# Attention and mixture of depths on one core: group 0's 1/rms by a ScalarE square root and a Newton step instead of GpSimd's power

## The chip, the core and the metric

The kernel runs on 1 core of one Trainium2 chip, in float32. The metric is the device time of one execution in microseconds (us), as the median of several runs. A core has five engines with queues of their own, each worked off in order: PE (TensorE, matrix products, with weight loads listed as PEld), DVE (VectorE), ACT (ScalarE), POOL (GpSimd) and SP (SyncE, which issues most DMAs). They wait for each other through semaphores only.

## What is computed

Normalized attention over 8 batches and 12 heads of 448 tokens with 64 dimensions, then a mixture-of-depths layer on the 768 joined columns. Cut to what matters here:

```python
def rmsnorm(x, g):
    rms = np.sqrt(np.mean(x * x, axis=-1, keepdims=True) + 1e-06)
    return x / rms * g
q_n, k_n = (rmsnorm(q, g_q), rmsnorm(k, g_k))
scale = 1.0 / np.sqrt(q.shape[-1])
scores = scale * np.matmul(q_n, k_n.transpose(0, 1, 3, 2))
scores = scores - np.max(scores, axis=-1, keepdims=True)
attn = np.exp(scores)
attn = attn / (np.sum(attn, axis=-1, keepdims=True) + 1e-09)
return np.matmul(attn, v).astype(np.float32)
...
for b in range(B):                       # x: attention output as (8, 448, 768)
    top_idx = np.argpartition(-scores[b], capacity)[:capacity]   # scores = x @ w_gate
    xe = x[b, top_idx]
    ye = np.maximum(xe @ w1, 0.0) @ w2
    out[b, top_idx] = x[b, top_idx] + g[:, None] * ye            # g = sigmoid(scores)
```

Each query and key row needs 1/sqrt(mean of squares + 1e-6). This is the quantity that the change computes in another way, for the first group only.

## The kernel before

The 96 heads are worked off in 24 groups of four (three groups to a batch). A group's 448 keys are cut into 7 blocks of 64, and one block of one group is a unit, numbered u = 7 n + i. For a unit, `scores` (L320) multiplies 64 keys with all queries of the four heads on PE into two PSUM tiles (`sc`, four buffers, hence two units at a time), and ScalarE takes the exponential of each out of PSUM (L337), with the keys' 1/rms as its per-row scale; no maximum is taken off. `values` (L345) multiplies the result with v and adds up over the 7 units. `add_probs` (L368) adds the exponentials on VectorE for the denominators.

The order of all work is written out by hand. The main loop at the end of `fast` issues, for each round q of four units, the scores of two units, the values of earlier units, then tasks and slots: `at(slot, fn)` puts a piece of work into the slot of a unit, `task(when, fn)` puts it at an opening. Each engine's queue holds its part in that order.

1/rms is made for each group from token-major copies of queries (i = 0) and keys (i = 1), the `tok` tiles of 448 KB. `squares` (L242) squares 128x896 elements on ScalarE into one of two buffers `sq`, whose 65th column holds 1e-6; `sum_squares` (L250) adds each row's 65 elements on VectorE (L255) and raises the sums to -0.5 on GpSimd (L256). For group 0's queries both work in two halves. The keys' result goes to the exponential as it is. The queries' result must lie along the free dimension: for groups 0 and 1, `scale_q_early` (L291) spreads it with 28 small products against an identity on PE (L298) into two `sc` tiles, and VectorE multiplies the transposed queries `qT` with it and with `gg`, the product of the two gains and the scale (L307). Later groups go through DRAM (`rows_out`, `rows_in`, L287).

The start, in program order: `Loads.__init__` (L29) sends the gain columns on ScalarE's queue and the first tokens and queries on SP's, and runs one small Exp (L40). `_build` (L1411) compares the gains with a bound on VectorE and all engines branch on the outcome (L1434 to L1436). `fast` then fills the `sq` columns, builds the identity on GpSimd, issues nine more loads on SP, builds `pick_pair` (a selection matrix for the denominators' products at L396) and `gg` on VectorE, and runs 13 transposes of the identity on PE (L169), whose result nobody reads. Then come group 0's squares and powers, group 1's squares, `scale_q_early(0)`, group 1's sums and powers, and the main loop, whose first opening holds `scale_q_early(1)`, after the scores of units 0 to 3 and the values of units 0 and 1. `prepare(n, slot)` places the squares and sums of groups 2 and up; those of group 2 lie in slots 0 to 3.

SP's queue works in order too: a load into a `tok` buffer waits until the squares of the tile that held it are done, and everything behind it on SP waits with it.

Of the kernel before, what the change touches and what calls it, by code (L numbers as in the profile page):

```python
# [10 lines left out]
F32 = mybir.dt.float32  # L11
I32 = mybir.dt.int32
AF = mybir.ActivationFunctionType
OP = mybir.AluOpType
AX = mybir.AxisListType
# [10 lines left out]
class Loads:  # L26


    def __init__(self, nc, pool, qT, kT, vp, tok, g2):  # L29
        self.nc, self.pool = nc, pool  # L30
        self.src = {"tok": tok, "qT": qT, "kT": kT, "v": vp}
        self.tiles = {}
        self.groups = tok.shape[1]
        self.gcol = pool.tile([128, 2], F32, name="gcol", bufs=1)
        nc.scalar.dma_start(out=self.gcol, in_=g2)
        neg_half = pool.tile([128, 1], F32, name="neg_half", bufs=1)
        nc.vector.memset(neg_half, -0.5)

        warm = pool.tile([128, 1], F32, name="warm", bufs=1)
        nc.scalar.activation(out=warm, in_=neg_half, func=AF.Exp)  # L40
        self.neg_half = neg_half
        self.load("tok", 0, 0)
        self.load("tok", 0, 1)
        self.load("qT", 0)

    def load(self, name, n, i=None):
        b, g = divmod(n, self.groups)
        src = self.src[name]
        if i is not None:
            src = src[b, g, :, i]  # L50
        elif name == "v":
            src = src[b, g]
        else:
            src = src[b, 2 * g : 2 * g + 2].rearrange("c p s -> p c s")
        pool = self.v_pool if name == "v" else self.pool
        bufs = {"tok": 6, "qT": 4, "kT": 3, "v": 3}[name]
        held = [key for key in self.tiles if key[0] == name]
        if len(held) == bufs:
            del self.tiles[held[0]]
        t = pool.tile(list(src.shape), F32, name=name, bufs=bufs)  # L60
        self.nc.sync.dma_start(out=t, in_=src)
        self.tiles[name, n, i] = t

    def get(self, name, n, i=None):
# [4 lines left out]
def fast(  # L69
# [21 lines left out]
    nc = tc.nc  # L91

    B, NP, _, S = loads.src["qT"].shape
    CP = 112
    NJ = S // CP
    D = 64
    NI = S // D
# [11 lines left out]
    scale = 1.0 / math.sqrt(D)  # L109
# [25 lines left out]
    sss, rinvs, bcs = {}, {}, {}  # L135
# [17 lines left out]
    load("v", 1)  # L153

    gg = const.tile([128, 1], F32, name="gg")

    pick_pair = const.tile([128, NJ // 2, 32], F32, name="pick_pair")
    nc.vector.memset(pick_pair, 0.0)
    for jj in range(NJ // 2):
        for c in range(2):  # L160
            r = 2 * jj + c
            nc.vector.memset(pick_pair[D * c : D * (c + 1), jj, r : r + 1], 1.0)
    nc.vector.scalar_tensor_tensor(
        out=gg, in0=loads.gcol[:, 0:1], scalar=scale, in1=loads.gcol[:, 1:2], op0=OP.mult, op1=OP.mult
    )

    ps = ps_moe.tile([128, 512], F32, tag="moe", name="warm_ps")
    for _ in range(13):
        nc.tensor.transpose(out=ps[:, 0:128], in_=ident, identity=ident)  # L169

    wg = const.tile([CP, DM], F32, name="wg")
# [70 lines left out]
    def squares(n, i):  # L242
# [4 lines left out]
        sss[n, i] = norm_pool.tile([128, 2, NI], F32, name="ss", bufs=4)  # L247
        return sq

    def sum_squares(n, i, sq):  # L250
        ss = sss.pop((n, i))
        rinv = norm_pool.tile([128, 2, NI], F32, name="rinv", bufs=8)
        flat = "p h i -> p (h i)"
        for h in [slice(0, 1), slice(1, 2)] if (n, i) == (0, 0) else [slice(0, 2)]:
            nc.vector.tensor_reduce(out=ss[:, h], in_=sq[:, h], axis=AX.X, op=OP.add)  # L255
            nc.gpsimd.tensor_tensor(  # L256
                out=rinv[:, h].rearrange(flat),
                in0=ss[:, h].rearrange(flat),
                in1=neg_half.to_broadcast([128, (h.stop - h.start) * NI]),
                op=OP.pow,  # L260
            )
        rinvs[n, i] = rinv

    def rows_out(n):
# [616 lines left out]
        while late:  # L881
            add_probs(late.pop(0))

    for i in range(2):
        sum_squares(0, i, squares(0, i))
    later = [squares(1, i) for i in range(2)]
    scale_q_early(0)
    for i in range(2):
        sum_squares(1, i, later[i])
    task((0, 0), scale_q_early, 1)  # L890

    def run(slots):
# [35 lines left out]
    while done < len(groups) or tasks:  # L928
        now[:] = q, 0
        k = PER * q  # L930
        for half in range(HALVES):
            for u in (k + 2 * half, k + 2 * half + 1):
                if u < units:
                    scores(u)
            run_values(k + 2 * half - 1, q)
        opening(q, 0)
        for half in range(HALVES):
            slots = (k + 2 * half, k + 2 * half + 1)
            early = bool(late)
            if early:  # L940
                spare[0] = True
                opening(q, 1)
                spare[0] = False
                add_late()
            if not short(q):
                run(slots)
            some = piece(q)
            spare[0] = not some and half == 0
            if not early and (some or half == 0 or len(tasks) > 2):
                opening(q, half + 1)  # L950
            spare[0] = False
            run(slots)
        q += 1
# [535 lines left out]
```

## Time and profile before

| What | us |
|---|---|
| Median of 3 runs | 518.45 (517.85 to 519.04) |
| The profiled execution | 513.42 |
| Its span, first to last instruction | 511.7 |
| PE busy | 491.6 (96%) |
| DVE busy | 354.0 (69%) |
| ACT busy | 274.8 (54%) |
| POOL busy | 187.0 (37%) |
| POOL powers L256, 49 of them | 135.7, of 128x14 2.83 each |
| ACT exponentials L337, 336 of them | 186.0, 0.641 each |
| ACT squares L246, 49 of them | 45.9, 0.949 each |
| DVE sums L255, 49 of them | 52.1, 1.074 each |
| HBM | 84.37 MB read, 28.50 MB written |

Busy times are sums over the whole span. PE's are modelled at their ends, so a PE that is busy throughout need not be at its peak. Every time in a timeline is counted from the first instruction of the span; a line there gives the start, the duration, the engine, the line of the code, the operation, output and input by name, the number of instructions merged into it, and in brackets how long the engine had been idle and what ended that.

### The profile page before, as it was taken

The page shows a single profiled execution, that of the slowest core. Times are in us where ns is not written, and L with a number is a line of the kernel's source. Part 1 is how long each engine was busy: PE and PEld are TensorE (multiplying, and loading weights), DVE is VectorE, ACT ScalarE, POOL GpSimd, SP SyncE. Part 2 cuts the span into 40 slices and gives each one's busy share as a digit, 9 for nine tenths or more (in the row PEclk, how much of TensorE's full clock was granted, in tenths as well). Part 3 has the DMA queues.
Part 4 walks back from the last instruction along what each step waited for, and adds up shares of the span by engine and source line. Part 5 has one row for each costly group of instructions (what it writes and reads, how often), then busy time and mean ns, then how long its engine had stood idle before and what let it go on. Part 6 is the DMA issues. An engine that isn't in the chain of part 4 may idle for free. (4 is left out here: it accounts for less than half of the span.)

```text
span 511.7 us, 11121 instructions
## 1 busy us (share of the span) xinstructions
PE 491.6 (96%) x4429; PEld 279.4 (55%) x4429; DVE 354.0 (69%) x670; ACT 274.8 (54%) x507; POOL 187.0 (37%) x104
## 2 busy tenths in 40 slices
PE   5999999988999999999999999999999899999994
PEld 4544445435555444666654454665554454786683
DVE  4566898699866898996687886777567686623201
ACT  4787886866757466665454737654634536310000
POOL 4694548444524174427123085036220022020102
PEclk9999999999999999999999999999999999999998
DMA  8977889999964673899461989567423318232601
GB/s 294 387 247 257 271 272 365 326 296 319 283 204 129 214 248 121 283 323 331 134 201 26 350 280 302 190 191 207 136 72 88 110 38 260 89 109 58 221 3 36
DMA packets 49295, 105.82 MB, mean 207 GB/s; under 512 B 11571, under 2 KB 26420, under 8 KB 49234
## 3 DMA queue, kind: packets, MB, share of 16 engines
q1 hardware_dynamic: 45826, 98.70, 59.9%
q0 software_dynamic: 3264, 6.31, 3.7%
q8 instruction: 37, 0.61, 0.5%
q14 instruction: 24, 0.20, 0.1%
q10 hardware_dynamic: 144, 0.00, 0.0%
HBM read 84.37 MB, written 28.50 MB: 221 GB/s over the span
## 5 line engine op out<-in xcount | busy, mean ns | idle before, releaser
L337 ACT ACTIVATE p<-sc,rinv 128x448 f32<-128x448 f32 x336 | 186.0, 641 | 88.3 <-PE sc L328 74.3
L256 POOL TENSOR_TENSOR rinv<-ss,neg_half 128x14 f32<-128x14 f32 (+1 forms) x49 | 135.7, 2775 | 184.4 <-DVE ss L255 164.9
L328 PE MATMUL sc<-qT,kT 64*64 64x448 f32 x1344 | 152.7, 545 | 1.0 <-DVE qT L307 0.8
L352 PE MATMUL av<-p,v 64*64 64x448 f32 x1344 | 147.0, 537 | 0.0
L368 DVE TENSOR_TENSOR sum<-sum,p 128x896 f32<-128x896 f32 x107 | 116.5, 1089 | 8.1 <-ACT p L337 1.9
L352 PEld LDWEIGHTS av<-p,v 64*64 64x64 f32 x1344 | 57.6, 133 | 69.6 <-issue 62.3
L328 PEld LDWEIGHTS sc<-qT,kT 64*64 64x64 f32 x1344 | 52.5, 132 | 69.3 <-issue 43.8
L255 DVE TENSOR_REDUCE ss<-sq 128x14 f32<-128x910 f32 (+1 forms) x49 | 52.1, 1074 | 11.9 <-ACT sq L246 11.6
L639 PE MATMUL moe_ps<-xeT,w 128*128 128x256 f32 (+1 forms) x288 | 56.1, 347 | 0.0
L539 POOL DMA_INDIRECT selected<-x,rank x32 | 35.8, 1118 | 47.7 <-DVE x L531 39.7
L639 PEld LDWEIGHTS moe_ps<-xeT,w 128*128 128x128 f32 x288 | 46.2, 191 | 6.8 <-issue 2.6
L246 ACT ACTIVATE sq<-tok 128x896 f32<-128x896 f32 (+1 forms) x49 | 45.9, 949 | 5.9 <-DMA tok<-in_tok_dram 5.6
L443 DVE TENSOR_TENSOR x<-x_ps,rden 112x512 f32<-112x512 f32 x48 | 32.5, 687 | 20.8 <-PE x_ps L441 18.3
L467 DVE SCALAR_TENSOR_TENSOR prod<-x,wg 112x256 f32<-112x256 f32 x96 | 40.6, 423 | 2.9
L587 POOL DMA_INDIRECT out_dram<-xe,row x10 | 10.5, 1052 | 85.7 <-DVE xe L596 67.9
L639 PE MATMUL sc<-xeT,w 128*128 128x256 f32 (+1 forms) x192 | 32.2, 328 | 0.3 <-ACT xeT L615 0.3
L441 PE MATMUL x_ps<-ident,xT 128*112 128x128 f32 x192 | 28.8, 276 | 2.0 <-DVE x L443 2.0
L639 PEld LDWEIGHTS sc<-xeT,w 128*128 128x128 f32 x192 | 28.8, 191 | 2.8 <-ACT xeT L615 0.5
L287 DVE SCALAR_TENSOR_TENSOR qT<-qT,gg,bc 128x896 f32<-128x896 f32 x22 | 25.3, 1149 | 4.4 <-DMA bc<-rows 4.4
L512 DVE SCALAR_TENSOR_TENSOR cmp<-score_rows,gate,earlier 112x448 f32<-112x448 f32 x32 | 21.9, 684 | 9.1 <-ACT score_rows L502 8.1
L441 PEld LDWEIGHTS x_ps<-ident,xT 128*112 128x112 f32 x192 | 21.8, 134 | 10.3 <-issue 4.5
L368 DVE TENSOR_TENSOR sum<-p 128x896 f32<-128x896 f32 x24 | 25.9, 1078 | 1.8 <-ACT p L337 1.8
(87 smaller groups left out, 331.9 us busy)
## 6 DMA issues: line engine op xcount, KB each, us to landing
tok<-in_tok_dram SPq DMA_DIRECT2D x48, 448.0 KB, 6.6
qT<-in_qT_dram SPq DMA_DIRECT2D x24, 448.0 KB, 6.6
kT<-in_kT_dram SPq DMA_DIRECT2D x24, 448.0 KB, 7.1
v<-in_vp_dram SPq DMA_DIRECT2D x24, 448.0 KB, 7.6
out_dram<-x SPq DMA_DIRECT2D x8, 1344.0 KB, 9.0
bc<-rows SPq DMA_DIRECT2D x44, 224.0 KB, 6.4
ring<-mixed SPq DMA_DIRECT2D x22, 384.0 KB, 5.3
xe<-selected SPq DMA_DIRECT2D x8, 385.0 KB, 3.7
```

The source lines that it names most:

```text
L246: nc.scalar.activation(out=sq[:, h, :, 0:D], in_=t[:, h], func=AF.Square, scale=scale)
L255: nc.vector.tensor_reduce(out=ss[:, h], in_=sq[:, h], axis=AX.X, op=OP.add)
L256: nc.gpsimd.tensor_tensor(out=rinv[:, h].rearrange(flat), in0=ss[:, h].rearrange(flat), in1=neg_half.to_broadcast([128, (h.stop - h.start) ...
L328: nc.tensor.matmul(out=scs[hh][D * c : D * (c + 1), 0:S], lhsT=get("kT", n)[r, c, D * i : D * (i + 1)], rhs=get("qT", n)[r, c, :], start=True,
L337: nc.scalar.activation(out=p[:, hh], in_=scs[hh][:, 0:S], func=AF.Exp, scale=rinvs[n, 1][:, hh, i : i + 1],)
L352: nc.tensor.matmul(out=avs[n][c][D * hh : D * (hh + 1), 0:S], lhsT=get("v", n)[r, hh, i, :], rhs=probs[u][r, hh], start=(i == 0), stop=(i ...
L368: nc.vector.tensor_tensor(out=sums[n], in0=probs.pop(u - 1) if begins else sums[n], in1=probs.pop(u), op=OP.add)
L441: nc.tensor.transpose(out=ps[:CP, j, :], in_=t[:, j, :], identity=ident)
L443: nc.vector.tensor_tensor(out=xs[b][:, :, col : col + 128].rearrange("p j (h d) -> p j h d", d=D), in0=ps[:CP].rearrange("p j (h d) -> p j ...
L467: nc.vector.scalar_tensor_tensor(out=prod[:, 0 : GH * D], in0=xs[b][:, j, cols], scalar=1.0, in1=wg[:, cols], op0=OP.mult, op1=OP.mult, ac ...
L539: w = nc.gpsimd.indirect_dma_start(out=t[:, :], out_offset=bass.IndirectOffsetOnAxis(ap=rank[:, j : j + 1], axis=0), in_=x[:, j, :], in_of ...
L639: nc.tensor.matmul(out=ps[:, i, :, :n], lhsT=w1[:, dc, 128 * (f0 + i) : 128 * (f0 + i + 1)], rhs=xeT[:, dc, 0:G, :n], start=(dc == 0), sto ...
```

## The change

For group 0 alone, the two powers on GpSimd (three instructions) are replaced. `sum_first` adds the squares as before; `root_first` takes the square root of the sums on ScalarE; `invert_first` takes its reciprocal on VectorE, y, and does one Newton step, y (1.5 - 0.5 s y y), in three more VectorE instructions. The small activation at the start is a Sqrt instead of an Exp. The first `tok` tile is loaded in two halves, the first on ScalarE's queue as its first instruction, the second on SP's. `pick_pair` and `gg` are built later, and there are 9 transposes at the start instead of 13. Group 1's squares, sums and powers no longer stand before the main loop but in it: queries behind the scores of unit 0, keys behind those of unit 2.

```diff
--- before.py
+++ after.py
@@ -32,14 +32,15 @@
         self.tiles = {}
         self.groups = tok.shape[1]
         self.gcol = pool.tile([128, 2], F32, name="gcol", bufs=1)
+        self.load("tok", 0, 0)
         nc.scalar.dma_start(out=self.gcol, in_=g2)
         neg_half = pool.tile([128, 1], F32, name="neg_half", bufs=1)
         nc.vector.memset(neg_half, -0.5)
 
-        warm = pool.tile([128, 1], F32, name="warm", bufs=1)
-        nc.scalar.activation(out=warm, in_=neg_half, func=AF.Exp)
+        warm = pool.tile([128, 2], F32, name="warm", bufs=1)
+        nc.vector.memset(warm, 1.0)
+        nc.scalar.activation(out=warm[:, 0:1], in_=warm[:, 1:2], func=AF.Sqrt)
         self.neg_half = neg_half
-        self.load("tok", 0, 0)
         self.load("tok", 0, 1)
         self.load("qT", 0)
 
@@ -58,7 +59,11 @@
         if len(held) == bufs:
             del self.tiles[held[0]]
         t = pool.tile(list(src.shape), F32, name=name, bufs=bufs)
-        self.nc.sync.dma_start(out=t, in_=src)
+        if (name, n, i) == ("tok", 0, 0):
+            for h, queue in enumerate((self.nc.scalar, self.nc.sync)):
+                queue.dma_start(out=t[:, h], in_=src[:, h])
+        else:
+            self.nc.sync.dma_start(out=t, in_=src)
         self.tiles[name, n, i] = t
 
     def get(self, name, n, i=None):
@@ -153,19 +158,9 @@
     load("v", 1)
 
     gg = const.tile([128, 1], F32, name="gg")
-
     pick_pair = const.tile([128, NJ // 2, 32], F32, name="pick_pair")
-    nc.vector.memset(pick_pair, 0.0)
-    for jj in range(NJ // 2):
-        for c in range(2):
-            r = 2 * jj + c
-            nc.vector.memset(pick_pair[D * c : D * (c + 1), jj, r : r + 1], 1.0)
-    nc.vector.scalar_tensor_tensor(
-        out=gg, in0=loads.gcol[:, 0:1], scalar=scale, in1=loads.gcol[:, 1:2], op0=OP.mult, op1=OP.mult
-    )
-
     ps = ps_moe.tile([128, 512], F32, tag="moe", name="warm_ps")
-    for _ in range(13):
+    for _ in range(9):
         nc.tensor.transpose(out=ps[:, 0:128], in_=ident, identity=ident)
 
     wg = const.tile([CP, DM], F32, name="wg")
@@ -247,18 +242,41 @@
         sss[n, i] = norm_pool.tile([128, 2, NI], F32, name="ss", bufs=4)
         return sq
 
+    def sum_first(i, sq):
+        ss = sss[0, i]
+        for h in [slice(0, 1), slice(1, 2)] if i == 0 else [slice(0, 2)]:
+            nc.vector.tensor_reduce(out=ss[:, h], in_=sq[:, h], axis=AX.X, op=OP.add)
+
+    def root_first(i):
+        root = norm_pool.tile([128, 2, NI], F32, name="ss", bufs=4)
+        nc.scalar.activation(out=root, in_=sss[0, i], func=AF.Sqrt)
+        return root
+
+    def invert_first(i, root):
+
+        ss = sss.pop((0, i))
+        rinv = norm_pool.tile([128, 2, NI], F32, name="rinv", bufs=8)
+        nc.vector.reciprocal(out=root, in_=root)
+        nc.vector.scalar_tensor_tensor(
+            out=rinv, in0=root, scalar=-0.5, in1=ss, op0=OP.mult, op1=OP.mult
+        )
+        nc.vector.tensor_tensor(out=rinv, in0=rinv, in1=root, op=OP.mult)
+        nc.vector.scalar_tensor_tensor(
+            out=rinv, in0=rinv, scalar=1.5, in1=root, op0=OP.add, op1=OP.mult
+        )
+        rinvs[0, i] = rinv
+
     def sum_squares(n, i, sq):
         ss = sss.pop((n, i))
         rinv = norm_pool.tile([128, 2, NI], F32, name="rinv", bufs=8)
         flat = "p h i -> p (h i)"
-        for h in [slice(0, 1), slice(1, 2)] if (n, i) == (0, 0) else [slice(0, 2)]:
-            nc.vector.tensor_reduce(out=ss[:, h], in_=sq[:, h], axis=AX.X, op=OP.add)
-            nc.gpsimd.tensor_tensor(
-                out=rinv[:, h].rearrange(flat),
-                in0=ss[:, h].rearrange(flat),
-                in1=neg_half.to_broadcast([128, (h.stop - h.start) * NI]),
-                op=OP.pow,
-            )
+        nc.vector.tensor_reduce(out=ss, in_=sq, axis=AX.X, op=OP.add)
+        nc.gpsimd.tensor_tensor(
+            out=rinv.rearrange(flat),
+            in0=ss.rearrange(flat),
+            in1=neg_half.to_broadcast([128, 2 * NI]),
+            op=OP.pow,
+        )
         rinvs[n, i] = rinv
 
     def rows_out(n):
@@ -881,12 +899,23 @@
         while late:
             add_probs(late.pop(0))
 
-    for i in range(2):
-        sum_squares(0, i, squares(0, i))
-    later = [squares(1, i) for i in range(2)]
+    sum_first(0, squares(0, 0))
+    root = root_first(0)
+    keys = squares(0, 1)
+    nc.vector.scalar_tensor_tensor(
+        out=gg, in0=loads.gcol[:, 0:1], scalar=scale, in1=loads.gcol[:, 1:2], op0=OP.mult, op1=OP.mult
+    )
+    invert_first(0, root)
+    sum_first(1, keys)
+    root = root_first(1)
     scale_q_early(0)
-    for i in range(2):
-        sum_squares(1, i, later[i])
+    invert_first(1, root)
+    nc.vector.memset(pick_pair, 0.0)
+    for jj in range(NJ // 2):
+        for c in range(2):
+            r = 2 * jj + c
+            nc.vector.memset(pick_pair[D * c : D * (c + 1), jj, r : r + 1], 1.0)
+    following = {0: (1, 0), 2: (1, 1)}
     task((0, 0), scale_q_early, 1)
 
     def run(slots):
@@ -932,6 +961,8 @@
             for u in (k + 2 * half, k + 2 * half + 1):
                 if u < units:
                     scores(u)
+                if u in following:
+                    sum_squares(*following[u], squares(*following[u]))
             run_values(k + 2 * half - 1, q)
         opening(q, 0)
         for half in range(HALVES):
```

## What I predict

> **What bounds the kernel now.** I read the windows by stage first, then the start in order of time, then the waits. The chain that ended last covers only the closing 8 us and says nothing about the start.
>
> ```profile
> core 0: us, PE busy (x) PEld busy (x) DVE busy (x) ACT busy (x) POOL busy (x), PEclk, DMA share, GB/s
> 0.00:13.00 13.00, 7.36 (x83) 6.12 (x85) 5.91 (x20) 5.39 (x7) 6.21 (x9) 1.00 0.81 296
> 13.00:20.00 7.00, 6.96 (x104) 3.53 (x98) 1.67 (x4) 6.21 (x10) 5.12 (x2) 1.00 1.03 397
> 20.00:40.00 20.00, 19.97 (x230) 10.31 (x232) 14.29 (x15) 15.79 (x29) 15.39 (x11) 1.00 0.76 263
> ...
> 100.00:120.00 20.00, 17.14 (x187) 7.69 (x183) 16.95 (x35) 15.08 (x29) 5.23 (x2) 1.00 1.02 304
> ```
>
> From 13 us on PE is busy nearly without a break (19.97 of 20 us, and so on to 100 us). So whatever the start gains or loses moves all later PE work and should arrive at the end almost whole. The change touches only the first 20 us. Their order of time:
>
> ```profile
> 1.19 1.28 ACT L40 ACT_TABLE_LOAD   x1 [1.19 <-PEq L1470]
> 2.48 0.20 ACT L40 ACTIVATE warm<-neg_half 128x1 f32<-128x1 f32 x1
> ...
> 4.98 1.05 ACT L246 ACTIVATE sq<-tok 128x448 f32<-128x448 f32 x2 [2.30 <-DMA tok<-in_tok_dram]
> 5.59 1.16 DVE L255 TENSOR_REDUCE ss<-sq 128x7 f32<-128x455 f32 x2 [0.74 <-ACT sq L246]
> 6.31 5.52 POOL L256 TENSOR_TENSOR rinv<-ss,neg_half 128x7 f32<-128x7 f32 x3 [1.73 <-DVE ss L255]
> 7.88 2.84 PE L298 MATMUL sc<-ident,rinv 64*64 64x64 f32 x56 [0.19 <-POOL rinv L256]
> 10.75 1.27 DVE L307 SCALAR_TENSOR_TENSOR qT<-qT,gg,sc 128x448 f32<-128x448 f32 x2 [2.15 <-PE sc L298]
> 13.15 4.48 ACT L337 ACTIVATE p<-sc,rinv 128x448 f32<-128x448 f32 x8 [0.76 <-PE sc L328]
> 17.52 1.99 ACT L246 ACTIVATE sq<-tok 128x896 f32<-128x896 f32 x2
> 19.38 1.27 DVE L307 SCALAR_TENSOR_TENSOR qT<-qT,gg,sc 128x448 f32<-128x448 f32 x2 [5.33 <-PE sc L298]
> ```
>
> The reader is to see two things. The first exponentials (13.15) wait for scores, not for the keys' 1/rms, whose power ended at 6.31 + 5.52 = 11.83. And they then run without a hole for 4.48 us: there ScalarE sets the pace, and PE, waiting for PSUM, follows.
>
> **Part 1, the start up to the spread.** Half of the first tokens is issued at about 0.78 instead of 1.20, the other half still at 1.20. Before, the square waited for the landing until 4.98; ScalarE, past the branch, could have begun at about 4.0. Its queue now holds one more DMA issue (0.37) ahead of the table load (1.28), which pushes its branch by some 0.1: square at 4.10. A rule speaks against this: the Trainium skill, "DMA: Bandwidth & Descriptors", section "Issuing engines are not separate DMA queues", says that transfers of several queues share the same 16 DMA engines and only issue time is saved. By it the second half lands 4.9 - 0.42 = 4.5, which its square, due 0.48 after the first (half of 1.05, overlapped), just does not feel; if the first half too came only then, 0.4 is lost. The trace's landing (4.9 for a whole tile issued at 1.20) cannot separate halves. I take 4.10, other end 4.50.
> Squares and sums take 6.75 - 4.98 = 1.77, so 5.87. The root, one ACTIVATE on 128x14, is near the 0.20 of warm: 6.13 with its hand-over. Four dependent VectorE operations on 128x14: the startup's small dependent operations (L1422 to L1427) follow one another at 0.25, those at L529 and L530 at 0.21; 3 x 0.25 + 0.17 = 0.92, other end 0.7. 1/rms of the queries: 7.09. The spread starts at 7.14, not 7.88: 0.74 gained. The nine warm-up transposes (3.01 / 13 = 0.23 each, from 4.68) end at 6.8 and are in no way.
>
> **Part 2, the spread gives half of it back.**
>
> ```profile
> 9.00:10.00 1.00, 1.00 (x24) 1.00 0.99 394
> 18.00:19.00 1.00, 1.00 (x47) 1.00 1.02 400
> ```
>
> These are PE windows: both show a granted clock of 1.00, yet in 18 to 19 us, nearly all spread of group 1, twice as many rows pass. Row starts in the trace are 0.107 per pair until 10.03, then 0.058. So the first spread was not waiting for the second power; it ran at PE's slow early pace and got its last half microsecond at the fast one. Starting earlier, all 28 pairs fall before 10.03 to 10.13: 7.14 + 28 x 0.107 = 10.13, plus 0.25 to drain. Scale (L307) at 10.4 instead of 10.75: gain 0.35.
>
> **Part 3, the first exponential.** In the changed order VectorE does the keys' Newton step behind both scales (next operation 1.19 after the first scale, as 10.75 to 11.94): 11.59 + 0.92 = 12.51. Squares, sum and root of the keys are done by 9 and hidden. ScalarE's table was loaded for Sqrt; a second load, for Exp, stands directly before the first exponential, behind the wait for that Newton result. Row: 1.28, and warm began at 2.48, at once. So the exponential starts at 12.55 + 1.28 = 13.83, **0.68 later** than 13.15. Scores (0.74 after the scale) are finished by then. The Trainium skill, "ScalarE: Activation LUTs", section "What ACT_TABLE_LOAD costs", prices a switch at 1.28 plus 1.38 of drain; by it 15.2, and the whole sum 1.4 more. I take the row: ScalarE has nothing in flight to drain here. GpSimd loses three powers, but none was on the path: nothing gained.
>
> **Part 4, group 1's squares.** Before, they lay at 10.32 and 11.45, in ScalarE's holes. Now they stand in its queue behind units 0 and 2 of the packed run. Let E be the first exponential. Unit 0 takes 1.05, the square 0.85 (pitch of one behind another at L246), so it ends at E + 2.0; sum 1.1 and power 2.58 (with hand-overs) give E + 5.8. Unit 1's exponentials end at E + 3.1, unit 2's at E + 4.1, the second square at E + 4.9, unit 3's at E + 6.0 (before: 4.48). On PE, unit 3's scores wait for unit 1's exponentials: E + 3.1 instead of 15.36 - 13.15 = 2.2, so both value units are done and the spread could start at E + 5.4. It waits for the power until E + 5.85 and needs 28 x 0.058 = 1.6: last row E + 7.42 instead of 19.12 - 13.15 = 5.97. **1.45 later.** Scores 4 and 5, the scale at 19.38 and the exponentials behind them all hang on it.
>
> **What is hidden.** pick_pair's five memsets (0.56) and gg go where VectorE waits. SP: the loads of group 3's tokens wait for group 1's squares (issued at 11.29 and 12.42, in each case as that square ended); they go to about 15.9 and 18.8, and queries, keys and values of group 2 behind them from 12.80 to 19. Six loads at 1.1 us are in by 27; group 2's queries are used at 32.63 + 2. The DMA engines were nearly idle around 25 to 27 us, so the room is there; were it not, the scale of group 2 would come late.
>
> **Sum:** -0.35 + (0.68 + 0.35) + 1.45 = 0.68 + 1.45 = +2.1. On the profiled execution's 513.42 (span 511.7) that is 515.5; the median shown, 518.45, is 5 above it, and I add the same: **520.5**.
>
> **Rivals.**
> 1. *The switch drains* (0.12): +2.1 + 1.4, 521.9. For it the skill's figure; against it warm's start at 2.48.
> 2. *PE's fast pace comes earlier* (0.18): if the spread ran at 0.058 throughout it would end at 7.14 + 1.62 + 0.22 = 9.0; scale and exponential are 1.4 earlier, total +0.7, 519.2: within 0.2%. For it: nothing shows what sets the turn at 10.03. Against: four fewer warm-ups cannot hasten it.
> 3. *A later stall is dissolved* (0.17), the faster side. One place:
>
> ```profile
> 102.48 1.15 DVE L287 SCALAR_TENSOR_TENSOR qT<-qT,gg,bc 128x896 f32<-128x896 f32 x1 [2.22 <-DMA bc<-rows]
> ...
> 108.04 0.40 PEld L441 LDWEIGHTS x_ps<-ident,xT 128*112 128x112 f32 x4 [1.88 <-DVE x L443]
> ...
> 116.18 0.35 PEld L396 LDWEIGHTS den_ps<-sum,pick_pair 128*32 128x32 f32 x16 [1.46 <-DVE sum L368]
> ```
>
> VectorE waits 2.22 for a broadcast in a full DMA queue, and PE pays 1.88 + 1.46 = 3.3 behind a late VectorE. If computing comes 2.1 later while the queue doesn't, all 3.3 vanish: 2.1 - 3.3 = -1.2, 517.2. It decides once the broadcast lands 2.2 earlier against VectorE. Against: SP's loads are issued as buffers come free, so the queue should move along with computing.
> That the change does less than it says I exclude: the changed order holds exactly one more table load and three powers less.
>
> **From cases to numbers.** Forecast 0.53 (own range 519.5 to 521.5). 0.2% is 1.04 us, about what a measurement of this kernel can tell from no change. Slower: nearly all of the forecast, rival 1, a little of rival 2: 0.65. Same: most of rival 2, edges of the others: 0.19. Faster: rival 3: 0.16. The range takes rival 1 and reaches down almost to rival 3: 517.5 to 522.4.
>
> **What would show it.** Square at 4.1, spread at 7.1 and ending near 10.4; an ACT_TABLE_LOAD of 1.28 right before the first exponential, at 13.8; the first sq of group 1 between exponentials; PE's second spread waiting for POOL, its scale near 21.5. I am wrong if the spread runs at the fast pace from the start, if the load stands earlier than the Newton result, or if the window 100 to 120 us shows PE busy for much more than 17.14.

## The result and the profile after

| | kernel before | changed kernel |
|---|---|---|
| Median of 22 runs each, taken together | 517.89 (513.88 to 520.69) | 518.99 (516.71 to 522.69) |
| Profiled execution | 513.42 | 517.81 |
| Its span | 511.7 | 516.1 |
| First exponential E | 13.15 | 13.24 |
| Exponentials of unit 4 | 20.15 | 21.62 |

All times are in us. The ratio of the times is 1.0043, with a 95% interval of 1.0020 to 1.0065: **slower by 2.2 us** (1.0 to 3.4). The difference of the two medians is only 1.1 and that of the two means 1.6, since both sets of runs are wide; part of the reason comes out of the experiments.

The start of the changed kernel in order of time (start, duration, engine, line, operation, and in brackets the idle time before it with what ended it):

```profile
3.92 1.05 ACT L241 ACTIVATE sq<-tok 128x448 f32<-128x448 f32 x2 [0.74 <-DMA tok<-in_tok_dram]
...
5.73 0.22 ACT L252 ACTIVATE ss<-ss 128x14 f32<-128x14 f32 x1 [0.76 <-DVE ss L248]
...
6.90 2.89 PE L316 MATMUL sc<-ident,rinv 64*64 64x64 f32 x56
...
9.82 1.27 DVE L325 SCALAR_TENSOR_TENSOR qT<-qT,gg,sc 128x448 f32<-128x448 f32 x2 [1.39 <-PE sc L316]
...
11.95 1.28 ACT L355 ACT_TABLE_LOAD   x1 [3.27 <-DVE pick_pair L913]
13.24 1.16 ACT L355 ACTIVATE p<-sc,rinv 128x448 f32<-128x448 f32 x2
...
14.29 0.95 ACT L241 ACTIVATE sq<-tok 128x896 f32<-128x896 f32 x1
...
15.13 2.21 ACT L355 ACTIVATE p<-sc,rinv 128x448 f32<-128x448 f32 x4
...
16.46 2.62 POOL L274 TENSOR_TENSOR rinv<-ss,neg_half 128x14 f32<-128x14 f32 x1 [11.91 <-DVE ss L273]
17.20 0.98 ACT L241 ACTIVATE sq<-tok 128x896 f32<-128x896 f32 x1
18.04 1.19 ACT L355 ACTIVATE p<-sc,rinv 128x448 f32<-128x448 f32 x2
...
19.13 1.42 PEld L316 LDWEIGHTS sc<-ident,rinv 64*64 64x64 f32 x52 [1.09 <-POOL rinv L274]
...
20.84 1.27 DVE L325 SCALAR_TENSOR_TENSOR qT<-qT,gg,sc 128x448 f32<-128x448 f32 x2 [1.53 <-PE sc L316]
...
21.62 1.16 ACT L355 ACTIVATE p<-sc,rinv 128x448 f32<-128x448 f32 x2 [0.72 <-PE sc L346]
```

The new way to 1/rms is quicker: the spread of the queries' 1/rms begins at 6.90, where it had begun at 7.88. The table for Exp is loaded a second time from 11.95 to 13.23, directly before the first exponential, and uses the gain up: E is 0.09 later. Then the two squares of group 1 stand between the exponentials, and the second spread (19.13) waits 1.09 for GpSimd's power. From E to the exponentials of unit 4 it takes 8.38 where it took 7.00. That adds 1.38, and unit 4 is 1.47 late.

The windows of the changed kernel (busy time of each engine, then granted clock, DMA share and GB/s) show where PE lost it:

```profile
core 0: us, PE busy (x) PEld busy (x) DVE busy (x) ACT busy (x) POOL busy (x), PEclk, DMA share, GB/s
...
13.00:20.00 7.00, 5.37 (x66) 2.51 (x68) 2.20 (x2) 6.99 (x13) 3.23 (x2) 1.00 0.88 314
...
100.00:120.00 20.00, 16.70 (x211) 7.99 (x207) 16.43 (x37) 13.43 (x27) 5.23 (x2) 1.00 1.05 305
```

Between 13 and 20 us PE now works 5.37 us instead of 6.96: it lost 1.59 in that stretch. Between 100 and 120 us it works 16.70 instead of 17.14: nothing was won back there, a little more was lost. The rows behind that second loss, the first of them from the kernel before:

```profile
108.04 0.65 PE L441 MATMUL x_ps<-ident,xT 128*112 128x128 f32 x4 [1.64 <-DVE x L443]
...
104.75 1.15 DVE L305 SCALAR_TENSOR_TENSOR qT<-qT,gg,bc 128x896 f32<-128x896 f32 x1 [2.65 <-DMA bc<-rows]
...
110.32 0.65 PE L459 MATMUL x_ps<-ident,xT 128*112 128x128 f32 x4 [2.08 <-DVE x L461]
```

VectorE's wait for the broadcast grew from 2.22 to 2.65, and the hole in PE that follows from 1.64 to 2.08. Laying the starts of all exponentials of the two traces side by side gives the lag of the changed kernel: 0.09 at unit 0, 1.47 at unit 4, 1.84 from 44 us on, 2.28 at 110 us. The step of 0.37 at 44 us lies at one operation of VectorE, which begins later behind the products that it waits for; first the kernel before, then the changed one:

```profile
41.55 1.29 DVE L443 TENSOR_TENSOR x<-x_ps,rden 112x512 f32<-112x512 f32 x2 [0.18 <-PE x_ps L441]
...
43.39 1.29 DVE L461 TENSOR_TENSOR x<-x_ps,rden 112x512 f32<-112x512 f32 x2 [0.55 <-PE x_ps L459]
```

PE's hole behind it is 0.59 instead of 0.22. All ten profiles of kernels with the change show this wait of 0.54 or 0.55, and the four of kernels without it 0.18; why, no run here shows.

Further steps beyond 130 us bring the spans to 4.4 apart. Of these, 1.84 arise between 183 and 431 us, and they cannot be put down to the change: set beside this first profile of the kernel before, nine of the profiles here, that of the same kernel with the weights later among them, lose 1.8 to 2.6 in that stretch, and the other four, that of the changed kernel's copy among them, 0.3 at most.

### The profile page after: what moved, and what is told of

Its sections match the earlier page's. It is cut to its first block, busy times and chain, and to the rows that moved or that the text cites. A ratio compares the mean times of both kernels' runs of the same rounds, so it can differ in the third digit from the quotient of the medians.

```text
span 516.1 us, 11122 instructions
## 1 busy us (share of the span) xinstructions
PE 492.8 (95%) x4425; PEld 279.1 (54%) x4425; DVE 355.6 (69%) x679; ACT 276.2 (54%) x510; POOL 182.1 (35%) x101
## 5 line engine op out<-in xcount | busy, mean ns | idle before, releaser
L274 POOL TENSOR_TENSOR rinv<-ss,neg_half 128x14 f32<-128x14 f32 x46 | 130.2, 2836 | 193.5 <-DVE ss L273 173.8
L273 DVE TENSOR_REDUCE ss<-sq 128x14 f32<-128x910 f32 x46 | 50.0, 1094 | 18.7 <-ACT sq L241 18.7
L459 PE MATMUL x_ps<-ident,xT 128*112 128x128 f32 x192 | 28.8, 276 | 2.7 <-DVE x L461 2.7
L459 PEld LDWEIGHTS x_ps<-ident,xT 128*112 128x112 f32 x192 | 21.8, 133 | 11.0 <-issue 4.5
```

The costliest lines, as they stand in the source:

```text
L273: nc.vector.tensor_reduce(out=ss, in_=sq, axis=AX.X, op=OP.add)
L274: nc.gpsimd.tensor_tensor(out=rinv.rearrange(flat), in0=ss.rearrange(flat), in1=neg_half.to_broadcast([128, 2 * NI]), op=OP.pow,)
L459: nc.tensor.transpose(out=ps[:CP, j, :], in_=t[:, j, :], identity=ident)
```

## Experiments

Each set of runs was made on one chip together with runs of the kernel before, whose median differed from set to set (514.61, 516.64, 515.96, and 517.60 beside the last kernel, which has a set of its own). A ratio is always to the runs of its own set. "Lag" is measured on the starts of exponentials in the profiles.

### First set: which part costs

**Copies of both kernels, one profiled execution each.** Before:

> The kernel before once more, for what one execution differs from another. In the two profiles the exponentials of unit 4 stand 1.47 us apart (20.15 and 21.62), those of unit 165 4.16 us, in steps near 40, 108, 130, 190 and 355 us. If the later steps are chance of single executions, this one keeps unit 0 at 13.15 and unit 4 at 20.15 within 0.1, and strays from the first profile by steps of 0.3 to 1 us after 40 us, of either sign. If they are a consequence of the change, it stays within 0.3 of the first profile to the end.

It took 512.47, with E at 12.83 and unit 4 at 19.82, both 0.33 earlier than in the first profile. After:

> The changed kernel once more. Chance: unit 0 at 13.24 and unit 4 at 21.62 within 0.1, later steps elsewhere or of another size. Consequence: unit 16 again 1.8 later than before, and the last units again some 4 us later.

It took 519.79, with E at 13.63 and unit 4 at 23.14, so 9.51 behind E and not 8.38. The windows of this copy of the changed kernel show why, in the column of the granted clock:

```profile
13.00:16.50 3.50, 2.05 (x11) 0.58 (x10) 0.83 (x1) 3.49 (x6) 0.00 (x0) 1.00 1.04 399
16.50:20.00 3.50, 3.50 (x21) 1.69 (x23) 1.37 (x2) 3.49 (x7) 2.83 (x2) 0.53 0.79 257
...
112.00:116.00 4.00, 3.34 (x20) 1.63 (x24) 3.78 (x7) 0.36 (x1) 2.31 (x1) 0.57 1.03 249
```

PE worked 2.05 of the 3.50 us up to 16.50, and then its clock was half from 16.73 to 20.14 by the trace's clock record. The same happened again from 112.30 to 115.71. So a start with holes in PE can cost more than the holes, and the price depends on the execution: three other profiles with these holes have unit 4 at 8.37 or 8.38 behind E and no fall of the clock there.

**Only group 1's squares later, in the kernel before.** Its powers, its single table and its whole first load stay:

```diff
-    later = [squares(1, i) for i in range(2)]
     scale_q_early(0)
-    for i in range(2):
-        sum_squares(1, i, later[i])
+    following = {0: (1, 0), 2: (1, 1)}
     task((0, 0), scale_q_early, 1)
...
                 if u < units:
                     scores(u)
+                if u in following:
+                    sum_squares(*following[u], squares(*following[u]))
```

> The kernel before with one part alone: group 1's squares, sums and powers behind the scores of units 0 and 2, powers on GpSimd for all groups, whole first load, no second table load. Theory A: unit 0 stays at 13.15, unit 4 goes from 20.15 to 21.6, PE's second spread waits for POOL, time 1.4 us (0.28%) above before. Theory B: unit 4 stays at 20.2 and the time too.

```profile
12.86 1.16 ACT L337 ACTIVATE p<-sc,rinv 128x448 f32<-128x448 f32 x2 [5.78 <-PE sc L328]
...
16.07 2.58 POOL L256 TENSOR_TENSOR rinv<-ss,neg_half 128x14 f32<-128x14 f32 x1 [4.18 <-DVE ss L255]
...
18.70 1.42 PEld L298 LDWEIGHTS sc<-ident,rinv 64*64 64x64 f32 x52 [1.04 <-POOL rinv L256]
...
21.19 1.16 ACT L337 ACTIVATE p<-sc,rinv 128x448 f32<-128x448 f32 x2 [0.67 <-PE sc L328]
```

In the order of time of this kernel one finds the same picture as in the changed one: the spread waits 1.04 for the power, and unit 4 comes 8.33 behind E, 1.33 more than the kernel before. Against the copy of the kernel before, which starts within 0.03 of it, unit 4 is 1.37 later. So the moved squares alone make the 1.38. The time, 516.30 (512.89 to 518.75, 10 runs), has a ratio of 1.0019 (0.9976 to 1.0063) and decides nothing by itself.

**The squares back in front, in the changed kernel.** All else of the change stays:

```diff
     root = root_first(1)
+    later = [squares(1, i) for i in range(2)]
     scale_q_early(0)
     invert_first(1, root)
+    for i in range(2):
+        sum_squares(1, i, later[i])
...
-    following = {0: (1, 0), 2: (1, 1)}
```

> The changed kernel with group 1's squares and sums back before the main loop, between the keys' root and the second table load. Theory A (group 1's squares inside the packed exponentials cost the 1.4; root, Newton step and table load are about even with the powers): the squares end at 12.4, the table load behind them at 13.7, unit 0's exponentials at 13.7 (half a microsecond later than now), unit 4 at 13.7 + 7.0 = 20.7, nearly 1 us before the changed kernel's 21.62, PE's second spread without a wait for POOL; time between the two kernels, some 0.5 above before. Theory B (the second table load costs it): unit 4 at 21.6 or later. Theory C (loads of group 3 held up on SP behind group 1's squares): unit 4 near 20.2, and later units lose nothing.

It took 518.44 (515.25 to 523.42, 10 runs); the ratio, without the run of 523.42, is 1.0075 (1.0031 to 1.0118). The numbers expected were missed, and the order of time tells why:

```profile
10.99 0.95 ACT L241 ACTIVATE sq<-tok 128x896 f32<-128x896 f32 x1 [1.24 <-DMA tok<-in_tok_dram]
...
12.12 0.95 ACT L241 ACTIVATE sq<-tok 128x896 f32<-128x896 f32 x1 [0.19 <-DMA tok<-in_tok_dram]
13.10 1.28 ACT L355 ACT_TABLE_LOAD   x1
...
14.39 2.21 ACT L355 ACTIVATE p<-sc,rinv 128x448 f32<-128x448 f32 x4
```

Group 1's tokens land only at about 11 and 12.1, the squares wait for them, and the table load stands in the queue behind the squares. E is at 14.39, and PE, which then had a hole from 12.4 to 15.1, ran at half clock from 14.71 to 18.12. Unit 4 came at 22.32. In the changed order the squares can't simply go back: with a table switch behind them, they hold up the first exponential.

### Second set: the table, one square, PE's holes

**The changed kernel unchanged, timed again.**

> The changed kernel timed beside the next three. Theory A (1.4 us from group 1's squares in the packed run, the rest even): 1.4 us above before at an equal granted clock. Theory D (on top of A: PE's holes at 13 to 19 us let the clock fall to half for 3.4 us in some executions, as the clock record of the second profile of this kernel showed at 16.7): the mean granted clock of its runs is on average below that of the runs of before, and the median lies more than 1.4 above.

518.24 (516.59 to 520.05, 10 runs), ratio 1.0027 (1.0002 to 1.0053). E at 13.25, unit 4 at 21.62, as before.

**The Exp table loaded in ScalarE's hole.** One exponential of one element, whose result nobody reads, right behind the keys' root (`warm` is kept as `loads.warm` for it):

```diff
     root = root_first(1)
+    nc.scalar.activation(out=loads.warm[:, 0:1], in_=loads.warm[:, 1:2], func=AF.Exp)
     scale_q_early(0)
```

> The changed kernel with one more Exp on one element directly behind the keys' root, which pulls the second table load from 11.95 to 8.7, into a hole of ScalarE. Theory A: unit 0's exponentials are then set by the scores, 2.4 behind the first scale, at 12.2 instead of 13.24, and unit 4 at 12.2 + 8.4 = 20.6, 1.0 earlier than now; time 0.5 above before. Theory B (the second table load is the loss): unit 4 at 20.2 or before and the time equal to before.

```profile
6.88 2.04 PE L316 MATMUL sc<-ident,rinv 64*64 64x64 f32 x56
...
9.95 1.28 ACT L911 ACT_TABLE_LOAD   x1
...
11.93 1.16 ACT L355 ACTIVATE p<-sc,rinv 128x448 f32<-128x448 f32 x2 [0.49 <-PE sc L346]
```

The order of time shows the load off the path: E is at 11.93, 1.31 earlier than in the changed kernel, and waits for scores. The spread took 2.04 instead of 2.89 in this execution, in which the clock record turns to full at 7.72 and not at 10.46 as in the profile of the changed kernel, and the first scale began at 9.60 instead of 9.82: that is 0.22 of the 1.31. The rest, 1.09, lies between the first scale and E: 2.33 here, 3.42 or 3.43 in the five profiles with the load right behind the Newton step, whatever the clock. Unit 4 is 8.38 behind E, as in the changed kernel. Yet the time is 518.67 (516.56 to 522.29, 10 runs), ratio 1.0037 (1.0007 to 1.0067): no gain from the earlier start can be seen in it.

**Besides, one square of group 1 in front.** The queries' square goes into ScalarE's hole, where its tokens have landed; the keys' square goes behind unit 3:

```diff
+    first = squares(1, 0)
     scale_q_early(0)
     invert_first(1, root)
+    sum_squares(1, 0, first)
...
-    following = {0: (1, 0), 2: (1, 1)}
+    following = {3: (1, 1)}
```

> As table_early, and group 1's queries squared before the exponentials, in ScalarE's hole behind the table load, its keys behind unit 3 instead of unit 2. Theory A: unit 0 at 12.3, units 0 to 3 packed without a square, unit 4 some 7.1 later at 19.4, that is 0.4 to 0.8 before the kernel before (19.82 and 20.15); PE's second spread without a wait for POOL; time at or 0.5 below before. Theory D adds: fewer holes on PE, so a granted clock like that of before.

E is at 12.06 and unit 4 at 19.41, **0.75 earlier than in the first profile of the kernel before** (0.42 earlier than in its copy); up to 104 us the exponentials run 0.57 to 0.95 ahead of the former. The time is 519.29 (516.8 to 522.72, 10 runs), ratio 1.0064 (1.0028 to 1.0100). So a start that beats the kernel before loses it again later. Where, the rows around 105 us and the windows show:

```profile
103.88 1.15 DVE L305 SCALAR_TENSOR_TENSOR qT<-qT,gg,bc 128x896 f32<-128x896 f32 x1 [4.19 <-DMA bc<-rows]
...
109.45 1.10 PE L459 MATMUL x_ps<-ident,xT 128*112 128x128 f32 x4 [3.63 <-DVE x L461]
```

```profile
100.00:110.00 10.00, 6.37 (x63) 3.08 (x56) 5.80 (x7) 5.39 (x10) 0.00 (x0) 0.92 1.04 312
110.00:120.00 10.00, 10.00 (x86) 4.04 (x88) 7.39 (x18) 5.34 (x11) 5.12 (x2) 0.74 1.02 276
```

VectorE waits 4.19 for the broadcast instead of 2.22, PE then stands 3.63 instead of 1.64, and the clock is half from 108.44 to 115.26. The four products of 128x128 take 1.10 instead of 0.65.

**PE's holes at the start filled with products that nobody reads,** to keep the clock up:

```diff
+    fill = {1: 5, 2: 2}
+    for _ in range(3):
+        nc.tensor.matmul(out=ps[:, 0:128], lhsT=ident, rhs=ident, start=True, stop=True)
     task((0, 0), scale_q_early, 1)
...
+                for _ in range(fill.pop(u, 0)):
+                    nc.tensor.matmul(out=ps[:, 0:128], lhsT=ident, rhs=ident, start=True, stop=True)
```

> The changed kernel with ten extra 128x128 products of the identity, whose result nobody reads, in PE's holes: three before the scores of unit 0, five behind those of unit 1, two behind those of unit 2. At the fast pace they take some 0.22 each, less than the holes. Theory A alone: the same time as the changed kernel. Theory D: no half clock between 13 and 21 us, unit 4 always 8.4 behind unit 0, and a higher mean clock and a shorter time than after_timed by some 0.5.

520.17 (516.22 to 523.07, 10 runs), ratio 1.0063 (1.0029 to 1.0097). The profile has no half clock, but the time is no shorter than that of the changed kernel, and the ten runs lie no closer together. So filling the holes at the start does not take the spread out of the times.

### Third set: the broadcasts behind a full DMA

From 80 to 120 us the DMA engines have no room left; this is the kernel before:

```profile
80.00:120.00 40.00, 36.92 (x440) 17.93 (x437) 33.45 (x65) 29.06 (x55) 19.44 (x10) 1.00 1.03 320
```

A DMA share of 1.03 says that the 16 engines are busy throughout. A broadcast issued at 93.5 lands at 102.5. Among what was issued ahead of it are loads of the second layer's weights. The next three kernels give those loads a slot that is 8 later, which puts two of them (768 KB) behind this broadcast:

```diff
-        at(16 + 3 * part, load_w, part)
+        at(16 + 3 * part + (8 if part >= NDC else 0), load_w, part)
```

**In the kernel before:**

> The kernel before with only the eight loads of the second layer's weights (384 KB each) given a slot that is 8 later, so that the two that went out ahead of the row broadcast of 93.5 us come behind it. Theory F (full DMA: between 80 and 120 us the 16 DMA engines are busy all the time, and VectorE's wait for the broadcast bc, 2.2 us at 100.3 to 102.5 in the kernel before, is the end of their backlog, so the landing moves with the bytes in front of it and not with the start): 768 KB less at the 320 GB/s of that stretch is 2.4 us, the wait at 100 to 103 us all but goes, the exponentials from 110 us on start about 2 us earlier, and the time is about 2 us less than before, 514 to 516 where before is 516 to 518. Theory G (a bound further back, the mixture's weights or the late tasks, sets the end): the wait goes but the time stays within 0.7 us of before, or grows if a product then waits for the weights.

```profile
101.73 1.15 DVE L287 SCALAR_TENSOR_TENSOR qT<-qT,gg,bc 128x896 f32<-128x896 f32 x1 [0.86 <-DMA bc<-rows]
...
107.43 0.65 PE L441 MATMUL x_ps<-ident,xT 128*112 128x128 f32 x4 [0.46 <-DVE x L443]
```

The wait shrinks from 2.22 to 0.86 and PE's hole from 1.64 to 0.46. The median is **513.71** (513.21 to 514.63, 12 runs), ratio 0.9929 (0.9900 to 0.9957): the lowest median of all kernels here. What is as telling is the width. Of the 29 runs of the kernel before in this set, 15 had a mean granted clock of 0.995 or more and took 513.9 to 515.96; the other 14 were below and took 517.12 to 520.59. With the weights later, all 12 runs were at 0.995 or more. So of the 2.25 between the medians about 1.1 goes with the shorter wait (513.71 against 514.78, the median of those 15), and the rest with a fall of the clock that no longer happens. Where the clock of the 14 fell is inferred: none of them was profiled. In the profile the gain is 1.18 at this broadcast, after 0.41 was lost at the one before it, where VectorE waits 3.38 instead of 1.01.

**In the changed kernel:**

> The changed kernel with the same eight loads 8 slots later. Theory F: VectorE's wait of 2.7 us for bc at 102.1 to 104.8 all but goes, and the kernel is about 2 us faster than the changed kernel, so about level with before (ratio 0.998 to 1.002), and still 1.5 to 2 us slower than the kernel before with the same edit, because the 1.47 us lost by unit 4 is then not touched by DMA at all. Theory G: ratio to before as without the edit, 1.003 to 1.004.

516.55 (515.92 to 519.86, 12 runs), ratio 1.0008 (0.9980 to 1.0036). So it is level with the kernel before, as theory F had it. Against the kernel before with the same edit it is **2.84 slower**, and the two sets of runs do not overlap: this is the clearest measure of the change. In the profiles 1.94 of it is there at unit 4 and 1.91 at the last unit and at the last operation of VectorE; the spans are 2.8 apart, and this last 0.9 arises at the last store of the output and behind it. Of the 1.94, 0.57 is there already at E: the first product of PE came 0.65 later in this execution, mostly because VectorE waited 1.74 instead of 1.14 for the row of gains that all engines branch on. Although the wait for the broadcast near 102 us is gone, four of the 12 runs had a mean clock below 0.995 (0.992 to 0.994).

**In the kernel with the early table and one early square:**

> The changed kernel with the exponentials' table loaded in ScalarE's hole, the queries of group 1 squared ahead of the exponentials, and the eight loads 8 slots later. In its profile without the last edit the exponentials ran 0.57 to 0.95 us ahead of the kernel before until 82 us, and VectorE's waits for bc were then 2.9 and 4.2 us (before: 1.0 and 2.2), after which the clock fell to half for 6.8 us. Theory F: with 768 KB less in front the waits shrink to 2 us at most, PE's hole at 106 to 109 us shrinks from 3.9 us and the clock holds, the lead of some 0.6 us lives beyond 115 us, and the time is 0.4 to 1 us below that of the kernel before with the same edit and about 3 us below before: the fastest of all. Theory G: no faster than before, ratio 1.003 to 1.007 as without the edit.

515.13 (514.16 to 516.24, 12 runs), ratio 0.9972 (0.9946 to 0.9997), where without the edit it was 1.0064. The mean clock was 0.995 or more in all 12 runs. But it is not the fastest. It leads the kernel before with the same edit by 0.85 to 0.91 at 21 to 39 us, by 0.46 from 44 to 87 us, and lags by 0.25 at 95 us and 0.38 from 109 us. The waits for the broadcasts in its order of time:

```profile
35.30 1.51 DVE L305 SCALAR_TENSOR_TENSOR qT<-qT,gg,bc 128x896 f32<-128x896 f32 x1 [4.60 <-DMA bc<-rows]
...
92.36 1.15 DVE L305 SCALAR_TENSOR_TENSOR qT<-qT,gg,bc 128x896 f32<-128x896 f32 x1 [4.10 <-DMA bc<-rows]
102.24 1.15 DVE L305 SCALAR_TENSOR_TENSOR qT<-qT,gg,bc 128x896 f32<-128x896 f32 x1 [1.11 <-DMA bc<-rows]
```

The step from lead to lag lies at the wait of 4.10. The kernel before with the same edit has 3.38 there: the broadcast lands at 92.4 in the one and at 92.1 in the other, though the one came 0.46 earlier up to there.

**And three loads of the first layer's weights 4 slots later too:**

```diff
-        at(16 + 3 * part + (8 if part >= NDC else 0), load_w, part)
+        at(16 + 3 * part + (8 if part >= NDC else 4 if part > 2 else 0), load_w, part)
```

> The run with the early table, one early square and the second layer's loads 8 slots later, and now also the last three loads of the first layer's weights (512 KB each) 4 slots later, so that the one of 75.3 us and one more go out behind the broadcasts of 76.7 and 68.5 us. Without this edit its exponentials led the kernel before with the same loads moved by 0.46 us up to 87 us and were 0.25 us behind at 95 us, after a wait of VectorE for bc of 4.1 us at 88.3 to 92.4. Theory F (the backlog of the DMA engines takes the lead away): 512 KB at 330 GB/s is 1.6 us, the wait at 92 us shrinks to some 2.5 us, 0.5 us or more of the lead lives on, and the time is about 0.7 us less, 514.4, level with the 513.7 of the kernel before with its loads moved within 1 us. Theory H (the lead is lost for another reason): 515 as without this edit.

517.94 (514.41 to 520.38, 12 runs), ratio 1.0005 (0.9984 to 1.0025). Both expectations on the time were missed. The waits moved:

```profile
90.14 1.15 DVE L305 SCALAR_TENSOR_TENSOR qT<-qT,gg,bc 128x896 f32<-128x896 f32 x1 [0.48 <-DMA bc<-rows]
104.95 1.15 DVE L305 SCALAR_TENSOR_TENSOR qT<-qT,gg,bc 128x896 f32<-128x896 f32 x1 [3.59 <-DMA bc<-rows]
```

The wait at 92 us went down to 0.48, more than expected: the broadcast landed 2.22 earlier (90.14), and VectorE came to it 1.40 later, E being 0.99 later in this execution (13.27), in which the clock turned to full only at 14.61. But two loads now go out behind that broadcast and in front of the next one, whose wait grew from 1.11 to 3.59: it was issued 1.50 later (95.22) and landed 2.71 later. PE's hole was 3.02, and the clock was half from 110.18 to 113.59; 7 of the 12 runs had a mean clock below 0.995. It looks as if the backlog was pushed along and not taken away; how much the later start added in this one profile is not separated.

### The wait and the clock over all profiles

The broadcast near 102 us in 14 profiles, sorted by the wait. The hole is PE's idle time ahead of the products of L441 (L459):

| kernel | VectorE's wait | PE's hole | clock at half behind it |
|---|---|---|---|
| changed, weights later | none | 0.46 | no |
| before, weights later | 0.86 | 0.46 | no |
| holes filled | 0.94 | 0.46 | no |
| early table and square, weights later | 1.11 | 0.58 | no |
| before, copy | 1.79 | 1.22 | no |
| before | 2.22 | 1.64 | no |
| squares back in front | 2.31 | 1.74 | no |
| changed | 2.65 | 2.08 | no |
| before, squares later | 2.92 | 2.35 | no |
| changed, timed again | 3.44 | 2.87 | no |
| changed, copy | 3.48 | 2.91 | 3.41 us |
| all weights later | 3.59 | 3.02 | 3.41 us |
| early table | 3.74 | 3.22 | 6.83 us |
| early table and square | 4.19 | 3.63 | 6.83 us |

At this place the clock fell behind each hole of 2.91 and more, and behind none of 2.87 or less. With two values so close the length alone can hardly decide, and at the start, with the squares back in front, it fell behind a hole of 2.6. The clock records show more: in each profile all turns and falls but the first turn lie a whole multiple of 3.413 us behind that turn (in the copy of the changed kernel full at 9.90, half at 16.73, full at 20.14, half at 112.30). Taken between the lines of this grid, the windows show how much PE worked (duration, then PE busy):

```profile
109.48:112.90 3.42, 1.79 (x20) 0.95 (x24) 3.32 (x6) 0.05 (x1) 0.76 (x1) 1.00 1.03 273
...
108.89:112.30 3.41, 0.86 (x8) 0.62 (x6) 3.10 (x5) 1.19 (x2) 0.00 (x0) 1.00 1.06 384
```

The first row belongs to the changed kernel timed again, whose hole of 2.87 is cut by a line at 109.48 into 1.24 and 1.63; the second to the copy, of whose hole of 2.91 2.55 lie within one window. Ahead of the four falls in the table PE worked 0.72 to 1.31 of such a window, ahead of the one with the squares in front 1.17; over the 14 profiles, between the first turn and 500 us, no other window has less than 1.64, and only one fall came behind more (2.02, at 16.73 in the copy). In the two cases of 6.83 us the clock stayed down for a second window, in which PE worked 2.29 and 2.40. So what counted in these runs is, with that one exception, how little PE worked in one window of the grid. That was read from the traces afterwards; no run was made to test it.

## Why the prediction was right, and where it was not

The time was forecast 2.1 us up, and it went up by 2.2 (1.0 to 3.4) by the ratio, by 1.1 between the medians. The forecast of 520.5 itself was 1.5 too high: the median of 518.99 lies in the range given, but below the 519.5 to 521.5 that it called its own. By its own steps:

- **The start up to the spread: right in kind, 0.2 too late.** Square at 3.92 (4.10 expected), spread at 6.90 (7.14). The second half's square followed without a wait, so the rule cited in the prediction, that two queues share the same DMA engines, was not felt by it; one load in one piece was not run beside it. In three of the ten profiles with the change, however, the row of gains that is issued at the same time (0.79) came late: VectorE waited 1.43 to 1.74 for it instead of 1.10 to 1.15 as in all others, and PE's first product was at 4.97 to 5.30 instead of 4.64 to 4.68. The prediction had no such term; that the half tile beside it is the reason is not shown.
- **The spread at the slow pace: right, and then 0.35 too long.** It took 2.89 for 56 products. The 0.25 added for draining was not there: the scale began at 9.82, at once, not at 10.4. In executions where the clock turned early the same 56 products took 2.04 (early table) and 2.20 (holes filled): rival 2's pace exists, but it goes with the execution and not with the change: in three profiles with one and the same start the clock turned at 7.82, 9.45 and 14.61.
- **The first exponential: right mechanism, wrong size.** The table load stood behind the keys' Newton step, took 1.28, and the exponential began 0.01 behind its end. Rival 1, the drain of 1.38 that the Trainium skill's "ScalarE: Activation LUTs" ("What ACT_TABLE_LOAD costs") prices, did not occur: ScalarE had been idle for 3.27, and load and exponential follow one another at 11.95, 13.24. But E came 0.09 later than before, not 0.68, because the two steps ahead of it were sized 0.6 too late together. That the load is what stands in the way is shown by the kernel with the early table: E 2.33 behind the first scale instead of 3.42.
- **Group 1's squares: right.** 1.45 expected, 1.38 in the first pair of profiles, 1.33 to 1.37 with nothing else changed.
- **"Should arrive at the end almost whole": only in part, and the hit of the total was partly luck.** At unit 4 the lag was 1.47 and not 2.1, the two terms of the start having been 0.6 too high. It did not stay as it was: every profile with the change adds 0.37 to 0.39 at 44 us, for which the prediction has no term, and in the first pair 0.44 came at the broadcast of 104.75. In the pair with the weights later 1.94 at unit 4 became 2.31 at 44 us and, because the kernel before then waited longer for a broadcast, 1.91 from 100 us to the last operation of VectorE; the times are 2.84 apart. So a start that was priced too high met losses that were not priced at all.
- **Rival 3, the late stall dissolved: refuted.** It needed the queue not to move along with a later computation. The broadcast was issued 2.63 later instead (96.14, was 93.51), and the wait grew to 2.65. (The 1.88 and 1.46 that it adds up are idle times of the weight loads; the holes of the products there were 1.64 and 1.22.) The argument against it on record, that SP issues loads as buffers come free, holds for a later start. For an earlier one it did not help: with E 1.1 earlier (early table and square) the broadcast was issued at 93.33 and landed 1.40 later than in the kernel before, and the wait took the lead away.

What stays open: the reason of the 0.37 at 44 us, the steps between 183 and 431 us, and the 0.9 at the last store. The worth of the halved first load alone was not tried.

## What to carry to other kernels

A faster way to a value gains only what the things put in its place leave over: here a quicker 1/rms bought 0.9 us at the scale (9.82 instead of 10.75), the table switch it needs, standing directly before the consumer, took 1.0 of that back (E 0.09 later), and two squares moved into packed exponentials cost another 1.4. In a case like this, put a table load into a hole with a one-element activation, and keep work out of the stretch where the engine runs without a hole. Before tuning a start, look for the next stretch in which the DMA engines are full: in these runs an earlier start came back as a longer wait as long as the transfers ahead of what is waited for were not thinned out, and 8 slots on one line of loads were worth more (2.25 us) than any reordering of the start that was tried.

## What the runs showed of the hardware

PE's clock was not settled here once it was up. By the trace's clock record it turns to full at 7.72 to 14.61 us in these executions, though PE's first product is at 4.64 to 5.30 in all of them, and the column of the granted clock shows 1.00 in windows before the turn; the pace of equal products shows it better (56 in 2.89 or in 2.04). Later it fell to half for 3.41 or 6.83 us, one or two steps of the grid of 3.413 us. The Trainium skill's "TensorE: Matmul & The Clock Gate" (Part 1) describes such a free-running window of about 3.4 us, and the same page ("Why this matters for your kernels") advises against idle gaps of more than about 3 us. The falls behind holes of 3.02 to 3.63 agree; those behind 2.91 and 2.6 came behind shorter ones, which filled most of one window. What the page does not lead one to expect is a fall after a window that was far from idle: PE had worked 2.02 of the 3.42 us before 16.73 in the copy of the changed kernel, and its clock was halved all the same.
